# Gate stores, token loads and first weights put at other places of the queues in a fused attention and gated-FFN kernel

## The chip, the cores and the metric

The kernel runs on one NeuronCore of one Trainium2 chip. The metric is the time in microseconds that the device takes for one execution. A profiled execution of the kernel before, with its trace, is what the reading below rests on. Engines are named as the profile names them: PE (TensorE matmul), PEld (its weight loads), DVE (VectorE), ACT (ScalarE), POOL (GpSimd) and SP (SyncE, which here issues nearly all DMAs, one after the other, in the order of the program).

## The reference

```python
# q, k, v: (8, 12, 448, 64) f32; w_pre, w_post: (12, 12); w_in: (768, 2048); w_out: (2048, 768)
scores = matmul(q, k.T) / 8                          # per batch and head
scores = einsum('bhij,hg->bgij', scores, w_pre)      # heads mixed before the softmax
attn   = softmax(scores, axis=-1)
attn   = einsum('bhij,hg->bgij', attn, w_post)       # and after it
x      = matmul(attn, v) -> (3584 tokens, 768)
h      = x @ w_in                                    # 3584 x 2048
g      = h - tanh(h)
return g @ w_out                                     # 3584 x 768
```

## The kernel before, in words

The attention takes the first 870 us or so and is not touched. Its results go to memory as tiles `xs`. The two products of the FFN follow in seven token blocks of 512. Each factor is split into a high and a low part, and a product is the sum of three matmuls (high x high, high x low, low x high).

**Block 0** is done in the plain way: sixteen steps `Block0.step`, one for each 128 columns of `w_in` (f = 0 to 15). A step loads the weights of f + 2 into one of three buffers `w0`, runs 18 matmuls of 512 columns (`products`), and copies the bank out. Every second step the *gate* `g = h - tanh(h)` of the last two column groups goes on: the class `Gate` has ACT parts `a1` (u, qa), `a2` (t, qb), `a3` (qb again) and DVE parts `d1` (two instructions), `d2`, `d3` (which writes g). The result is stored to `go`. `load_all_xq` loads the *token tiles* b11l, b21l, t3l, b22l, t4l of the next pair of blocks.

**Blocks 1 to 6** are taken in three pairs s = 0, 1, 2 by a scheme with seven products in place of eight. `xq_jobs` is a generator of the *token sums*: it subtracts token tiles on DVE into `xr`, casts the high parts on ACT (`high`) and subtracts for the low parts on DVE (`low`); `next(xq)` does the next job. `pair_step(s, q, ...)` runs for q = 0 to 7; in it come seven products of nine matmuls each, with right sides b11, b21, t2, t1, t3, b22, t4, into two PSUM banks X and Y. I call the code around product i *slot i*. Product i first loads the weights of product i + 6 (`more_wa`, seven buffers `wa`), so that load waits until product i - 1 has read its buffer. X is written by products 0, 2, 4, 6, and Y by 1, 3, 5: product 4 adds onto X, and so waits until ACT has copied X out into h23 after product 2. `Late` holds the second half of the gate work of the step before, cut into v0 to v4, which stand in slots 0 to 4. The seven gate sums of a step are in one tile `g` with one buffer; they are stored to `gs` (1.75 MB) and the next step's v0 writes `g` again.

**The second product** (`w_out`) is cut into *units* of 12 matmuls (`Results`): 32 plain ones for block 0, then 56 for each pair. Units are called between the products (`res.units`); before a new weight tile or gate tile is used, its loads (`w2`, `gl`) are issued two ahead, and every second unit casts a gate tile into gh on ACT and gl on DVE (`parts`). HELD units are kept for the *joint* between two pairs, where there are no products of the first kind, and AHEAD units of the new pair are taken there in advance. At a joint v0 to v4 come one by one, each with one token-sum job and one unit.

Every engine carries out its instructions in the order in which the code calls them (`in_order`). The pools `plain` (w0 and the tokens xh, xl of block 0) are closed after block 0, and `wa`, `w2b` and `cb` take their place.

## Time and profile before

| | |
|---|---|
| three runs, median (range) | 1839.65 us (1835.8 to 1841.04) |
| the profiled execution: time, span of the core | 1841.15 us, 1839.4 us |
| busy: PE, PEld, DVE, ACT, POOL | 1696.6, 1410.8, 1215.5, 1148.1, 404.0 us |
| moved by DMA | 477.42 MB, 260 GB/s on the mean |
| DMA issues after the attention that are named below | gs<-g: 24 of 1792 KB; go<-g: 8 of 512 KB; w<-wi: 16 of 768 KB; wa: 168 of 384 KB |

The profile's times are microseconds from the start of the span. A row of the windows view gives for a stretch the busy time of each engine (with its number of instructions), then the granted clock of PE (1.00 is full speed), the share of DMA and its rate. A row of the timeline gives start, duration, engine, line, what is written and read, and in brackets how long the engine had been idle and what ended that. A row of the waits view gives who waited for whom: total, times, longest.

### The profile page before, as it was taken

The numbers are of one execution on the slowest core, as the hardware profiler recorded it, in microseconds if no ns is written. First come the engines' busy times: TensorE is split into PE (matmuls) and PEld (weight loads), VectorE is DVE, ScalarE is ACT, GpSimd is POOL, SyncE is SP. The second block draws the span as 40 slices with busy tenths as digits, with TensorE's granted clock in tenths as the row PEclk, the third lists the DMA queues.
The fourth block names the chain that finished last, engine by engine and source line by source line (L and its number), as shares of the span: only waits on it lengthen the run. The fifth ranks groups of instructions, "written<-read, shape, count | busy, mean of one in ns | idle before, by whom it ended". The sixth has DMA issues, their size and how long they took to land.

```text
span 1839.4 us, 40980 instructions
## 1 busy us (share of the span) xinstructions
PE 1696.6 (92%) x16068; PEld 1410.8 (77%) x16068; DVE 1215.5 (66%) x2119; ACT 1148.1 (62%) x2016; POOL 404.0 (22%) x574
## 2 busy tenths in 40 slices
PE   8999999999998999999776999789999699998998
PEld 6777777777776777777654888678888589888998
DVE  5676777666676677764365878848777857777333
ACT  5777877776887687775355666545666455665232
POOL 1354555454545455551000000000000000000000
PEclk9999999999999899999887999989999899999999
DMA  8768798787978689775556778787979779786997
GB/s 183 213 212 258 239 252 248 226 239 220 260 247 230 211 245 262 227 236 180 197 183 223 255 286 304 262 312 276 351 288 369 272 268 350 299 318 248 333 321 279
DMA packets 337743, 477.42 MB, mean 260 GB/s; under 512 B 103824, under 2 KB 262288, under 8 KB 337552
## 3 DMA queue, kind: packets, MB, share of 16 engines
q1 hardware_dynamic: 337244, 474.38, 78.2%
q8 instruction: 128, 2.10, 0.5%
q14 instruction: 63, 0.52, 0.1%
q10 hardware_dynamic: 308, 0.43, 0.1%
HBM read 277.09 MB, written 120.59 MB: 216 GB/s over the span
## 4 chain that ended last, share of the span: by engine, by line
PE 67%; DMA 12%; DVE 8%; ACT 6%; issue 3%; POOL 2%; SPq 2%; ACTq 0%; DVEq 0%; POOLq 0%
PE ps_o L929 12%; PE ps_m L971 8%; PE ps_p L890 7%; PE ps_h L315 6%; PE ps_h L316 6%; PE ps_h L318 5%; PE y L523 5%; PE ps_q L846 5%; PE y L525 5%; PE y L524 5%; DMA t<-s 2%; DMA gs<-g 2%; DMA w<-wo 1%; DMA vr<-in_v_dram 1%; PE ps_m L812 1%
## 5 line engine op out<-in xcount | busy, mean ns | idle before, releaser
L929 PEld LDWEIGHTS ps_o<-wr,e 60*112 60x112 f32 (+1 forms) x5760 | 307.7, 176 | 42.8 <-POOL wr L912 18.4
L929 PE MATMUL ps_o<-wr,e 60*112 60x60 f32 (+1 forms) x5760 | 316.4, 260 | 15.8 <-ACT at L939 7.0
L899 DVE TENSOR_REDUCE mx<-ps_p 128x1 f32<-128x448 f32 x360 | 207.9, 619 | 178.2 <-PE ps_p L890 177.8
L901 ACT ACTIVATE e<-ps_p,mx 128x448 f32<-128x448 f32 x360 | 225.4, 633 | 92.5 <-DVE mx L899 90.4
L523 PE MATMUL y<-w,gh 128*128 128x384 f32 x672 | 231.6, 345 | 39.8 <-DMA w<-wo 20.0
L525 PE MATMUL y<-w,gl 128*128 128x384 f32 x672 | 230.8, 343 | 7.2 <-DVE gl L438 7.2
L524 PE MATMUL y<-w,gh 128*128 128x384 f32 x672 | 230.0, 342 | 0.0
L438 DVE TENSOR_TENSOR gl<-gl,gh 128x1024 fp32r<-128x1024 f32 x92 | 112.6, 1224 | 172.3 <-ACT gh L437 172.2
L939 ACT COPY at<-ps_o 112x960 f32<-112x960 f32 x156 | 153.9, 987 | 82.7 <-PE ps_o L929 82.1
L890 PE MATMUL ps_p<-t,wpre 60*64 60x448 f32 (+1 forms) x1440 | 181.0, 570 | 13.2 <-DMA t<-s 11.0
L971 PEld LDWEIGHTS ps_m<-at,vr 112*64 112x64 f32 x3072 | 152.4, 140 | 34.6 <-ACT at L946 13.0
L971 PE MATMUL ps_m<-at,vr 112*64 112x120 f32 (+1 forms) x3072 | 167.2, 266 | 11.2 <-ACT at L946 5.2
L523 PEld LDWEIGHTS y<-w,gh 128*128 128x128 f32 x672 | 130.0, 193 | 46.6 <-ACT b22h L565 13.8
L437 ACT CAST gh<-gl 128x1024 fp32r<-128x1024 f32 x92 | 96.0, 1044 | 110.5 <-DMA gl<-gs 78.3
L912 POOL TENSOR_TENSOR wr<-wpost,zs 128x120 f32<-128x120 f32 x180 | 70.7, 393 | 329.6 <-DVE zs L911 226.5
L525 PEld LDWEIGHTS y<-w,gl 128*128 128x128 f32 x672 | 129.8, 193 | 8.7 <-DVE gl L438 8.6
L524 PEld LDWEIGHTS y<-w,gh 128*128 128x128 f32 x672 | 129.9, 193 | 3.7
L846 PE MATMUL ps_q<-kk,qh 64*120 64x448 f32 (+1 forms) x768 | 123.7, 399 | 1.2 <-DVE kk L798 0.5
L846 PEld LDWEIGHTS ps_q<-kk,qh 64*120 64x120 f32 (+1 forms) x768 | 59.9, 176 | 82.8 <-issue 51.4
L851 DVE COPY s<-ps_q 120x448 f32<-120x448 f32 (+1 forms) x192 | 112.5, 615 | 11.9 <-PE ps_q L846 10.6
L331 ACT ACTIVATE u<-h 128x1024 f32<-128x1024 f32 x56 | 59.5, 1063 | 95.7 <-DVE h L688 77.8
L347 ACT ACTIVATE qb<-u,bias 128x1024 f32<-128x1024 f32 x56 | 64.7, 1155 | 68.4 <-DVE qa L344 68.2
(174 smaller groups left out, 3349.1 us busy)
## 6 DMA issues: line engine op xcount, KB each, us to landing
t<-s SPq DMA_DIRECT2D x342, 210.0 KB
gs<-g SPq DMA_DIRECT2D x24, 1792.0 KB
gl<-gs SPq DMA_DIRECT2D x84, 512.0 KB
w<-wo SPq DMA_DIRECT2D x52, 768.0 KB
wa<-ss SPq DMA_DIRECT2D x96, 384.0 KB
w<-ts SPq DMA_DIRECT2D x48, 768.0 KB
wa<-wi SPq DMA_DIRECT2D x72, 384.0 KB
cr<-in_moe_w_in_dram SPq DMA_DIRECT2D x48, 256.0 KB
```

What stands on the lines that cost most here:

```text
L438: nc.vector.tensor_sub(lo, raw(lo), raw(hi))
L523: nc.tensor.matmul(y, gh[:, tok], wh, start=first, stop=False, skip_group_check=True)
L524: nc.tensor.matmul(y, gh[:, tok], wl, start=False, stop=False, skip_group_check=True)
L525: nc.tensor.matmul(y, gl[:, tok], wh, start=False, stop=last, skip_group_check=True)
L846: nc.tensor.matmul(ps[:n, :S], qx[a, hp, :], kx[a, hp % 2], start=(x == 0), stop=(x == 2))
L851: eng(sts[i][:n, 2 * hp + j, :], ps[:n, :S])
L890: nc.tensor.matmul(pss[r][halves[j], :], wpre[k, :], ts[j][k, :], start=True, stop=True)
L899: nc.vector.tensor_reduce(out=mx, in_=ps, axis=AX.X, op=ALU.max, negate=True)
L901: nc.scalar.activation(e, ps, AF.Exp, bias=mx, scale=1.0, accum_out=zs[:, 0, r : r + 1])
L929: nc.tensor.matmul(ps[:CP, j, c * GP : (c + 1) * GP].rearrange("p (h i) -> p h i", i=GI)[:, :, r * GH : (r + 1) * GH], e[k, c * CP : (c + ...
L939: nc.scalar.copy(ats[i0][:, :, :, at : at + 2 * GI].rearrange("p c h (j i) -> p j (c h) i", j=2), ps[:CP, :, : NC * GP].rearrange("p j (x ...
L971: nc.tensor.matmul(pv[j * D : (j + 1) * D, r, :n], vt[:, j, c, :], ats[i][:, c, 2 * hp + j, :n], start=(c == 0), stop=(c == NC - 1),)
```

## The change

1. *Block 0:* the store of a gate to `go` is no longer issued in its own step but in the next one, behind that step's weight load (`self.store`); two more steps are issued ahead of the flush that ends the attention; the token loads are spread over the steps f = 3 to 7, the loads of w2 and gl over f = 10 to 15, the token sums over even f from 6 (five jobs, where there were seven); the new pools are opened right behind the matmuls of f = 15, with `w2b` at the first place and `wa` behind it.
2. *Every pair step:* `copy_predicated` is cut off from `d3` as `d4`; v3 (a3 and d3) now stands in slot 2 ahead of the copy of X, d4 of the second half in slot 3, the sums in slots 3 and 4; the store to `gs` is issued in slot 6.
3. *Joints:* the gate parts come first and the token sums behind them; five of eleven token-sum jobs are done there, and the other six in slots 0 to 4 of the pair's first step (two in slot 0); the store of the last `g` comes after ten units; AHEAD is 6 instead of 4, and each of seven places has two units; `int(due + 1e-6)` mends the rounding of the units.

```diff
     def close_plain():
         ff.plain.close()
-        ff.wap, ff.w2b, ff.cb = pool("wa", 7, "left"), pool("w2b", 1, "left"), pool("cb", 9, "left")
+        ff.w2b, ff.wap, ff.cb = pool("w2b", 1, "left"), pool("wa", 7, "left"), pool("cb", 9, "left")
...
         def d3(self, out):
             nc.vector.tensor_mul(out, self.qa, self.u)
+
+        def d4(self, out):
             nc.vector.copy_predicated(out, self.qb.bitcast(I32), self.t)
...
-        def step(self):
+        def step(self, between=None):
...
             if f + 2 < NF:
                 load_w0(f + 2)
+            if self.store:
+                self.store()
+                self.store = None
+            if between:
+                between(f)
             if f < NF:
                 ph = hbank()
                 products(ph, ff.w.pop(f), [ff.x[c] for c in range(NK)], True, True)
+                if f == NF - 1:
+                    close_plain()
+                    more_wa(6)
...
-                    nc.sync.dma_start(gos[:, f - 3 : f - 1], g)
+                    old.d4(g)
+                    self.store = lambda: nc.sync.dma_start(gos[:, f - 3 : f - 1], g)
...
         sub("t3l", "b11l")
+        yield
         both("b11")
...
         low("t1", xr)
+        yield
         sub("b22l", xr)
...
         def v2(self):
             self.g2.d1()
+
+        def v3(self):
             self.g2.d2()
-
-        def v3(self):
+            self.g2.a3()
+            self.g2.d3(self.g[:, 2:4])
+
+        def v4(self):
             g = self.g
-            self.g2.a3()
-            self.g2.d3(g[:, 2:4])
+            self.g2.d4(g[:, 2:4])
             nc.vector.tensor_add(g[:, 4:6], g[:, 0:2], g[:, 2].unsqueeze(1).to_broadcast([P, 2, TB]))
 
-        def v4(self):
+        def v5(self):
             g = self.g
             nc.vector.tensor_add(g[:, 6], g[:, 1], g[:, 4])
             nc.vector.tensor_add(g[:, 2], g[:, 3], g[:, 6])
-            nc.sync.dma_start(gss[self.s][:, :, self.q], g)
+
+        def store(self):
+            nc.sync.dma_start(gss[self.s][:, :, self.q], self.g)
...
         product(2, X, False)
         if late:
             late.v2()
+            late.v3()
         h23 = work("h23")
         nc.scalar.mul(h23[:, 0], X, -1.0)
...
         g1.a3()
+        if late:
+            late.store()
         rest(6)
...
+        for _ in range(2):
+            block0.step()
         now()
...
-    load_all_xq(0, ("b11l", "b21l", "t3l", "b22l", "t4l"))
...
+    def between0(f):
+        if 3 <= f <= 7:
+            load_all_xq(0, (("b11l", "t3l", "b21l", "b22l", "t4l")[f - 3],))
+        if f in (10, 12):
+            res.more_w2((f - 10) // 2)
+        if f in (13, 15):
+            res.more_gr((f - 13) // 2)
+        if 6 <= f < NF and f % 2 == 0:
+            next(xq, None)
+
     while block0.f < NF + 2:
-        block0.step()
-        if 3 <= block0.f < NF + 1 and block0.f % 2:
-            next(xq, None)
-        if block0.f == NF - 2:
-            res.more_w2(1)
-        if block0.f == NF:
-            close_plain()
-            more_wa(6)
+        block0.step(between0)
+    block0.store()
     res.more_w2(2)
-    res.more_gr(1)
...
-    HELD, AHEAD = 8, 4
+    HELD, AHEAD = 8, 6
...
             def between(i):
-                next(xq, None)
+                for _ in range(1 + (i == 0)):
+                    next(xq, None)
...
-        for f in (late.v0, late.v1, late.v2, late.v3, late.v4):
-            f()
-            next(xq, None)
-            res.units(1)
+        jobs = [
+            [late.v0], [late.v1, late.v2], [late.v3], [late.v4], [late.v5, partial(next, xq, None)],
+            [partial(next, xq, None)] * 2 + [late.store], [partial(next, xq, None)] * 2,
+        ]
+        for fs in jobs:
+            for f in fs:
+                f()
+            res.units(2)
         late = None
-        if s + 1 < NS:
-            for _ in range(HELD + AHEAD - 5):
-                next(xq, None)
-                res.units(1)
```

On SP at the start of block 0 the order before is as follows (xs<-x is the last store of the attention, w<-wi a weight load of block 0, here that of f = 3; the first gate's store comes three rows further down).

```order
L738 DMA xs_64<-x 768x1x208
L556 DMA b11l<-xs_58 128x3x384
L556 DMA b11l<-xs_59 128x3x128
L556 DMA b21l<-xs_58 128x3x384
L556 DMA b21l<-xs_59 128x3x128
L556 DMA t3l<-xs_59 128x3x320
L556 DMA t3l<-xs_60 128x3x192
L556 DMA b22l<-xs_59 128x3x320
L556 DMA b22l<-xs_60 128x3x192
L556 DMA t4l<-xs_58 128x3x384
L556 DMA t4l<-xs_59 128x3x128
L308 DMA w_13433<-wi_66 128x1536
```

With the change the same queue holds:

```order
L308 DMA w_13397<-wi_66 128x1536
L308 DMA w_13419<-wi_67 128x1536
L760 DMA xs_64<-x 768x1x208
L308 DMA w_13473<-wi_67 128x1536
L567 DMA b11l<-xs_58 128x3x384
L567 DMA b11l<-xs_59 128x3x128
L308 DMA w_13503<-wi_68 128x1536
L388 DMA go<-g 128x1024
L567 DMA t3l<-xs_59 128x3x320
L567 DMA t3l<-xs_60 128x3x192
L308 DMA w_13540<-wi_68 128x1536
```

The weight loads of f = 3 and 4 moved ahead of the attention's last store, the five token tiles stand one by one behind a weight load each, and the store to go stands behind one.

In a pair step (s = 0, q = 3) SP and ACT read before, first SP from the weight loads of slots 3 and 4 to the store, then ACT from slot 0 to slot 3:

```order
L613 DMA wa_14339<-ss3_80 128x768
L613 DMA wa_14355<-ss3_80 128x768
L644 DMA gs0_90<-g_14286 896x1x512
L613 DMA wa_14386<-ss3_80 128x768
L613 DMA wa_14404<-ss3_80 128x768
```

```order
L663 COPY h01_14450<-ps_h_14437 128x512
L331 ACTIVATE u_14453<-h23_14323 128x1024
L332 ACTIVATE qa_14454<-u_14453,bias_13124 128x1024
L336 ACTIVATE t_14472<-h23_14323 128x1024
L337 ACTIVATE qb_14471<-u_14453,bias_13124 128x1024
L678 ACTIVATE h23_14489<-ps_h_14437 128x512
L347 ACTIVATE qb_14471<-u_14453,bias_13124 128x1024
L684 ACTIVATE h01_14450<-ps_h_14438 128x512
```

and with the change (names as before; lines have moved by 9 to 20):

```order
L626 DMA wa_14341<-ss3_80 128x768
L626 DMA wa_14355<-ss3_80 128x768
L626 DMA wa_14385<-ss3_80 128x768
L626 DMA wa_14403<-ss3_80 128x768
L663 DMA gs0_90<-g_14286 896x1x512
```

```order
L682 COPY h01_14450<-ps_h_14437 128x512
L331 ACTIVATE u_14453<-h23_14325 128x1024
L332 ACTIVATE qa_14454<-u_14453,bias_13124 128x1024
L336 ACTIVATE t_14472<-h23_14325 128x1024
L337 ACTIVATE qb_14471<-u_14453,bias_13124 128x1024
L347 ACTIVATE qb_14471<-u_14453,bias_13124 128x1024
L698 ACTIVATE h23_14491<-ps_h_14437 128x512
L704 ACTIVATE h01_14450<-ps_h_14438 128x512
```

The store moved behind the weight loads of slots 5 and 6, and on ACT a3 (the second qb) moved ahead of the copy of X into h23.

At the first joint DVE reads with the change, from the old pair's v0 (d3, d4) on; rows L572 and L579 are token sums, L449 the low part of a gate tile:

```order
L353 COPY_PREDICATED g<-qb,t 128x1024
L449 TENSOR_TENSOR gl<-gl,gh 128x1024
L340 SCALAR_TENSOR_TENSOR qa<-qa,h_15152 128x1024
L341 TENSOR_TENSOR t<-h_15152,t 128x1024
L344 SCALAR_TENSOR_TENSOR qa<-qb,qa 128x1024
L350 TENSOR_TENSOR g<-qa,u 128x1024
L449 TENSOR_TENSOR gl<-gl,gh 128x1024
L353 COPY_PREDICATED g<-qb,t 128x1024
L655 TENSOR_TENSOR g<-g 128x1024
L659 TENSOR_TENSOR g<-g 128x512
L660 TENSOR_TENSOR g<-g 128x512
L572 TENSOR_TENSOR xr<-t3l,b11l 128x1536
```

Before, three token-sum rows (L561, L568) stood between v0's last row and the second half's d1; now none stands there, and the rows of t2, t4, t3 and b22 follow inside the next pair step.

More of the change, by code (lines that the diff above doesn't have):

```diff
@@ L356, in __init__ @@
         def __init__(self):
-            self.f, self.old = 0, None
-        def step(self):
+            self.f, self.old, self.store = 0, None, None
+        def step(self, between=None):
             f, old = self.f, self.old
@@ L625, in v0 @@
             self.g1.d3(self.g[:, 0:2])
+            self.g1.d4(self.g[:, 0:2])
         def v1(self):
@@ L682, in pair_step @@
         if late:
-            late.v3()
+            late.v4()
         nc.scalar.mul(h01[:, 0], Y, -1.0)
@@ L689, in pair_step @@
         if late:
-            late.v4()
+            late.v5()
         g1 = Gate(h01)
@@ L1305, in kernel_body @@
                 due += per_step / 7
-                units.append(int(due))
-                due -= int(due)
+                units.append(int(due + 1e-6))
+                due -= units[-1]
             late = pair_step(s, p, late, units, between)
```

## The prediction

> **What bounds the kernel now.** I read the engines' busy time, then windows by stage, then what PE waited for, then the queues there.
>
> ```profile
> PE 1696.6 (92%) x16068; PEld 1410.8 (77%) x16068; DVE 1215.5 (66%) x2119; ACT 1148.1 (62%) x2016; POOL 404.0 (22%) x574
> 888.40:1015.67 127.27, 87.14 (x334) 69.30 (x334) 75.42 (x59) 67.41 (x71) 0.00 (x0) 0.81 0.59 209
> 1015.67:1160.27 144.60, 143.23 (x684) 119.35 (x683) 119.59 (x117) 93.43 (x102) 0.00 (x0) 1.00 0.80 287
> 1160.27:1239.03 78.76, 58.05 (x280) 51.89 (x279) 44.83 (x36) 35.81 (x47) 0.00 (x0) 0.87 0.80 280
> 1239.03:1420.76 181.73, 181.73 (x899) 162.94 (x899) 140.53 (x136) 112.39 (x128) 0.00 (x0) 1.00 0.87 319
> 1420.76:1496.54 75.78, 55.78 (x268) 50.80 (x267) 49.29 (x44) 31.34 (x30) 0.00 (x0) 0.89 0.80 288
> 1496.54:1678.24 181.70, 181.70 (x899) 162.91 (x899) 138.89 (x135) 113.68 (x132) 0.00 (x0) 1.00 0.82 301
> 1678.24:1839.40 161.16, 144.18 (x793) 141.82 (x791) 62.03 (x64) 47.76 (x55) 0.00 (x0) 0.96 0.85 303
> ```
>
> PE bounds it. The seven stretches are: the entry (block 0 from f = 3, and the first step of pair 0); pair 0's other seven steps, up to the end of their last product; joint 1 with the first step of pair 1; pair 1's other steps; joint 2 with a first step; pair 2's other steps; joint 3 to the end. In the pairs' steps PE is full; it idles 40 us at the entry and 21, 20 and 17 at the joints, and there its clock is low besides. No matmul goes away, so all gain must come from these four places, and the full steps can only lose. Pair 0's row has 69 groups (a product, or a unit of as many columns): 143.23 / 69 = 2.08 us a group, and twice that, 4.1, for the 18 matmuls of a block-0 product.
>
> ```profile
> PE ps_h L315 <- DMA w<-wi: 22.0, 4, 10.2
> PE ps_h L315 <- DMA wa<-wi: 13.5, 1, 13.5
> 881.42 1.75 SPq L556 DMA_DIRECT2D b11l<-xs  x2
> 889.49 2.27 SPq L308 DMA_DIRECT2D w<-wi  x3
> 898.58 0.77 PE L315 MATMUL ps_h<-xh,w 128*128 128x512 f32 x1 [10.17 <-DMA w<-wi]
> 947.96 0.32 SPq L377 DMA_DIRECT2D go<-g  x1
> 948.37 1.21 SPq L308 DMA_DIRECT2D w<-wi  x2
> 953.71 0.76 PE L315 MATMUL ps_h<-xh,w 128*128 128x512 f32 x1 [5.12 <-DMA w<-wi]
> 981.39 0.32 SPq L377 DMA_DIRECT2D go<-g  x1
> 981.82 1.20 SPq L613 DMA_DIRECT2D wa<-wi  x2
> 986.27 0.76 PE L315 MATMUL ps_h<-b11h,wa 128*128 128x512 f32 x1 [13.49 <-DMA wa<-wi]
> ```
>
> The large entry waits have one form: SP stands at a store whose gate is not done, or at five token loads, and the weight load behind it goes out late; alone it lands 5.3 us after its issue (948.37 to 953.71).
>
> **The entry.** Ahead of the stores, a weight load goes out when its buffer has been read, two products (8.2 us) before it is needed. It can still queue behind a token load and a gate store: 768 + 768 + 512 KB at the 319 GB/s of the fullest row are 6.6 us, with issue and landing about 8. So nearly all 22.0 go; I leave 4 us of waits on the 13 products. The first `wa` load stands behind the gate of f = 10, 11, which is done about 1 us after product 14; the load lands some 7 us after that product, 3 after the last. The first pair step's product 0 then starts at 888.4 + 13 x 4.1 + 4 + 3 = 949 against 986.27.
>
> But that step has lost its cover: ACT and DVE still owe two gates, and six token-sum jobs have moved into it. The rows that price this, and the ring of the next part:
>
> ```profile
> L565 ACT CAST t2h<-xr x2: 1471/1476/1482, 1185.2 to 1443.8; 128x1536 fp32r<-128x1536 f32 x2
> L568 DVE TENSOR_TENSOR t2l<-xr,t2h x2: 1751/1752/1753, 1188.9 to 1447.6; 128x1536 fp32r<-128x1536 f32 x2
> L438 DVE TENSOR_TENSOR gl<-gl,gh 128x1024 fp32r<-128x1024 f32 x92 | 112.6, 1224 | 172.3 <-ACT gh L437 172.2
> L437 ACT CAST gh<-gl 128x1024 fp32r<-128x1024 f32 x92 | 96.0, 1044 | 110.5 <-DMA gl<-gs 78.3 <-PE y L524 26.5 <-DMA gl<-go 3.1
> 1095.51 0.53 SPq L644 DMA_DIRECT2D gs<-g  x1
> 1103.03 1.23 DVE L350 TENSOR_TENSOR g<-qa,u 128x1024 f32<-128x1024 f32 x1 [3.06 <-DMA gs<-g]
> 1104.36 1.06 ACT L331 ACTIVATE u<-h 128x1024 f32<-128x1024 f32 x1 [2.73 <-DVE g L350]
> 1104.36 1.41 DVE L351 COPY_PREDICATED g<-qb,t 128x1024 f32<-128x1024 int32 x1
> 1106.63 1.23 DVE L340 SCALAR_TENSOR_TENSOR qa<-qa,h 128x1024 f32<-128x1024 f32 x1 [0.29 <-ACT qa L332]
> 1108.91 1.22 DVE L344 SCALAR_TENSOR_TENSOR qa<-qb,qa 128x1024 f32<-128x1024 f32 x1
> 1109.09 0.60 ACT L678 ACTIVATE h<-ps_h 128x512 f32<-128x512 f32 x1 [0.49 <-DVE t L341]
> 1109.74 0.50 PE L315 MATMUL ps_h<-t3h,wa 128*128 128x512 f32 x1 [0.83 <-ACT h L678]
> 1110.17 1.15 ACT L347 ACTIVATE qb<-u,bias 128x1024 f32<-128x1024 f32 x1 [0.48 <-DVE qa L344]
> 1115.38 0.84 PE L318 MATMUL ps_h<-b22h,wa 128*128 128x512 f32 x3
> ```
>
> A gate costs DVE 3 x 1.22 + 1.23 + 1.41 = 6.3 us, and two of them in turn with ACT's parts end about 11 us after product 15. t2's low part (1.48 on ACT, 1.75 on DVE) comes behind: product 2 waits 6.5. The unit behind it needs gl, which stands on DVE behind t2's and t4's low parts and two subtractions of 1.75 each: 5.5. t3 is cast only when product 3 is copied out: 0.6 + 1.48 + 1.75 = 3.8 ahead of product 4. b22 is cast behind slot 4's a1: a subtraction of 0.7, 1.06, 1.15, 1.48 and 1.75 make 6.1, less a unit of 2.08: 4. Together 19.8, and 4 for slow clock: the step lasts 20.8 + 23.8 and ends at 993 or 994, not 1015.67. **Entry: -22.** Bounds: -33 (half of the step's waits gone) and -10 (weight loads still late by 4 us every third time).
>
> **Pair 0's steps: the store.** Here the change adds a wait. There is a ring: d3 (L350) cannot write g before the store has landed, 7.5 us after its issue; u waits for d3, and so on to ACT's copy of X (L678), for which product 4 (t3) waits. Before, product 4 comes 6.7 us after d3 starts. The change moves both ends. First, a3 (L347) now stands ahead of the copy, and itself waits for d2 (L344): copy and product come at 1110.17 + 1.15 + 0.6 instead, 8.85 after d3. Second, the store goes out behind slot 6's weight load, which waits for the end of product 5 (b22): 1115.38 + 0.84 - 1109.74 = 6.5 after product 4 starts, and 0.5 for issue. The ring is 8.85 + 6.5 + 0.5 + 7.5 = 23.4 us; PE's step of ten groups is 20.8. From the second store on, product 4 waits 2.6 in each of six steps: 15.6, less the 1.4 idle of before. The clock adds:
>
> ```profile
> 1696.24:1699.65 3.41, 1.37 (x9) 1.05 (x8) 2.49 (x3) 0.00 (x0) 0.00 (x0) 1.00 0.24 89
> 1699.65:1703.07 3.42, 3.42 (x12) 3.42 (x11) 0.00 (x0) 0.00 (x0) 0.00 (x0) 0.50 1.03 370
> ```
>
> 2.04 us of idle within 3.41 were followed by 3.42 at half clock. By the place of a 2.6 us wait in such a stretch about 6 in 10 would do so, at 1.7 us inside the ring: some 5. **+19.5.** Bounds: 0 (the store lands sooner than in the rows above) and +30 (a landing of 9.7, below).
>
> The Trainium skill ("TensorE: Matmul & The Clock Gate", section "Why this matters for your kernels") has it that PE idle below about 3 us does not lower the clock; by it the clock would add nothing here. The two rows above speak against it.
>
> **Pairs 1 and 2.** A step has 12 or 13 groups, 25 to 27 us, so the ring has room, but not in each step. Where a unit stood in slot 4, product 5 ends 10 groups into its step: 20.9 + 0.5 + 7.5 less 25 is d3 at 4 us into the next. Where gl is made in slot 0 there, casts and sums (1.04 + 1.22 + 0.7) push the copy of X to 11.8 after d3; in slot 1, behind ACT's t and qb, to 13.2. Product 4 is due after 7 groups, at 14.6. By the order two steps of a pair then wait 1.2 and two 2.6; with the clock 9.5. Two units fewer stand in these steps (-4.2): **+5.3 for each pair.** Bounds: -4 and +13.
>
> **The joints.**
>
> ```profile
> PE y L523 <- DMA w<-wo: 13.6, 1, 13.6
> PE y L523 <- ACT qb L337: 8.7, 1, 8.7
> PE y L525 <- DVE gl L438: 5.1, 3, 3.6
> ```
>
> At joint 1 (first row) a pair's last store waits on SP ahead of the next weights; at joint 2 (the others) v0 and the token sums alternate on DVE, and PE waits. Now that store is behind the loads, and DVE makes four gl among ten gate instructions and four sums: 24.6 us from d3, which starts 6 us after the last product; the loads behind eight output stores hold the last two units to about 34. PE has 15 groups, 31 us. So the next pair's product 0 comes 38 us after the last product, against 78.8 - 25 = 53.8. Its first step has the t3 and b22 waits of the entry, partly under units: 25 + 8.4, and 2 for clock. **Joint 1: 73.3 for 78.8, -5.5; joint 2 by the same sum 73, -2.8** (it has three units more than before). Joint 3 has no token sums: of 17 us idle and some 5 of slow clock 16 stay, and one unit goes: **-8.** All three together could give -30 (no idle left) or +5 (weights still late).
>
> Loads and sums that only change places cost the same; the cover is block 0's matmuls, and its price without them is the entry's lower bound. The pools' new order only changes which buffer a load waits for: the first two `wa` then wait for f = 13 in place of 15, which is in the 3 us above.
>
> **The sum.** -22 + 19.5 - 5.5 + 5.3 - 2.8 + 5.3 - 8 = -8: 1833 us against the profiled execution's 1841.15 (span 1839.4). The median of the runs is 1.5 lower: **1832**. What a measurement of this kernel tells from no change is 0.3%, 5.5 us.
>
> **The rivals.**
> - *The store lands later still (slower).*
>
> ```profile
> 1414.67 0.53 SPq L644 DMA_DIRECT2D gs<-g  x1
> 1424.33 1.23 DVE L350 TENSOR_TENSOR g<-qa,u 128x1024 f32<-128x1024 f32 x1 [2.48 <-DMA gs<-g]
> ```
>
> Here, with token loads around it, it took 9.7. Each us of landing costs six steps of pair 0 and eight of the others, 14 us. At 9.1 it is +22: 1854; from 8.1 on there is no gain. For it: two weight loads now stand straight ahead of the store. Against it: the 7.5 above had two right behind. 0.23.
> - *The loads stay the bound (no change).* DMA is already 0.80 to 0.87 busy in the pairs; if the joints give half and block 0's loads come 1.5 us later each second time, 1840. 0.24.
> - *The ring does not bind,* because the store lands while DVE is busy anyway: pair 0 at 0, the others at -4 each: 1795 to 1804. The 3.06 of wait ahead of d3 speaks against it. 0.09.
> - *Short waits leave the clock alone:* 5 + 2 x 2.3 + 2 less: 1820. The page named above gives this rule. 0.08.
>
> **The numbers.** The forecast's own case (1815 to 1846) has 0.36. Faster: 0.31 of it, the last two rivals, and 0.04 of the second: 0.52. No change: 0.18 of the second, 0.04 of the first case and 0.02 of the store's: 0.24. Slower: the rest, 0.24. The range, 1804 to 1855, reaches the rivals on both sides.
>
> **What would show it.** Right: product 0 near 950; idle ahead of t2, t3 and b22 in each pair's first step; 2 to 3 us ahead of t3, ended by ACT's copy, in six steps of pair 0, with d3 waiting for gs; product 0 some 38 us behind the last product at joints 1 and 2. Wrong: steps of pair 0 still 20.8 long, or weight loads of block 0 still waited for by 5 us and more.

## Result, and the profile after

The changed kernel takes 1882.2 us (median of four runs, 1879.1 to 1885.1) against 1839.65 for the kernel before, the median of its three runs (a fourth, disturbed one took 3230 us and is left out): a ratio of 1.0236, 95% interval 1.0204 to 1.0267. It is 2.4% slower, where 1832 was forecast and 1855 was the upper end. The profiled execution took 1885.07 us (span 1883.3), 43.9 more than the one of before. The page's line of busy times, the windows of the same seven stretches (columns as in the prediction), and the waits of PE from f = 3 on (smaller rows left out):

```profile
PE 1724.8 (92%) x16068; PEld 1419.0 (75%) x16068; DVE 1214.6 (64%) x2119; ACT 1146.1 (61%) x2016; POOL 403.4 (21%) x574
```

```profile
891.66:1000.28 108.62, 86.51 (x334) 67.19 (x333) 75.60 (x60) 68.25 (x72) 0.00 (x0) 0.87 0.71 253
1000.28:1167.17 166.89, 149.85 (x684) 123.45 (x683) 119.37 (x116) 93.17 (x102) 0.00 (x0) 0.96 0.74 256
1167.17:1248.18 81.01, 65.83 (x303) 56.99 (x303) 46.06 (x36) 36.49 (x47) 0.00 (x0) 0.85 0.76 269
1248.18:1445.39 197.21, 183.65 (x875) 161.40 (x875) 137.74 (x134) 110.05 (x127) 0.00 (x0) 0.97 0.82 293
1445.39:1528.23 82.84, 64.69 (x303) 57.83 (x303) 52.16 (x46) 34.94 (x37) 0.00 (x0) 0.90 0.78 277
1528.23:1725.60 197.37, 183.88 (x875) 161.36 (x875) 137.65 (x134) 110.19 (x127) 0.00 (x0) 0.97 0.77 274
1725.60:1883.30 157.70, 139.12 (x780) 135.73 (x779) 60.82 (x63) 46.61 (x54) 0.00 (x0) 0.98 0.86 300
```

```profile
PE ps_h L315 <- ACT h L698: 37.2, 15, 5.1
PE y L534 <- DMA w<-wo: 14.0, 6, 5.8
PE y L534 <- ACT gh L448: 12.1, 3, 7.9
PE ps_h L315 <- ACT b22h L576: 10.6, 3, 4.4
...
PE ps_h L315 <- DMA w<-wi: 3.4, 3, 1.4
```

The entry is shorter: block 0's weight loads are waited for 3.4 us in place of 22.0. But the pairs' steps, full before, are so no longer. The largest wait is now on L698, ACT's copy of X, ahead of product 4. By the prediction's steps, in us against before:

| step | forecast | measured |
|---|---|---|
| entry, to the end of the first pair step | -22 | -15.4 (1000.28 for 1015.67) |
| pair 0, steps 1 to 7 | +19.5 | +22.3 |
| joint 1 and first step | -5.5 | +2.3 |
| pair 1, steps 1 to 7 | +5.3 | +15.5 |
| joint 2 and first step | -2.8 | +7.1 |
| pair 2, steps 1 to 7 | +5.3 | +15.7 |
| joint 3 to the end | -8 | -3.5 |
| sum | -8 | +43.9 |

The timeline of one long step (step 3 of pair 1) shows the way from the store to product 4. The columns are start, duration, engine, line and operation; in brackets the idle time before it and what ended it.

```profile
1293.44 0.32 SPq L428 DMA_DIRECT2D gl<-gs  x1
1293.81 0.42 SPq L418 DMA_DIRECT2D w<-ts  x1
1295.52 0.32 SPq L626 DMA_DIRECT2D wa<-ss  x1
1295.93 0.56 SPq L663 DMA_DIRECT2D gs<-g  x1
...
1306.45 1.23 DVE L350 TENSOR_TENSOR g<-qa,u 128x1024 f32<-128x1024 f32 x1 [5.69 <-DMA gs<-g]
...
1307.77 1.06 ACT L331 ACTIVATE u<-h 128x1024 f32<-128x1024 f32 x1 [5.29 <-DVE g L350]
...
1317.70 1.15 ACT L347 ACTIVATE qb<-u,bias 128x1024 f32<-128x1024 f32 x1 [4.76 <-DVE qa L344]
1318.75 0.58 ACT L698 ACTIVATE h<-ps_h 128x512 f32<-128x512 f32 x1
...
1319.38 0.79 PE L315 MATMUL ps_h<-t3h,wa 128*128 128x512 f32 x1 [5.10 <-ACT h L698]
```

The store goes out at 1295.93; d3 (L350) stands ready on DVE for 5.69 us and starts when the store has landed, 10.5 us after its issue; u (L331) waits for d3; a3 (L347) and behind it the copy (L698) come 11.3 and 12.3 us after d3, and PE has stood 5.10 us. In the list of what waited for the store's line, the changed kernel's row comes first, then the row of the kernel before (us, times).

```profile
  DVE g L350: 73.4, 21
```

```profile
  DVE g L350: 18.8, 14
```

### The profile page after: what moved, and what is told of

It reads as the page before. It is cut to its first block, busy times and chain, and to the rows that moved or that the text cites. A ratio compares the mean times of both kernels' runs of the same rounds, so it can differ in the third digit from the quotient of the medians.

```text
span 1883.3 us, 40937 instructions
## 1 busy us (share of the span) xinstructions
PE 1724.8 (92%) x16068; PEld 1419.0 (75%) x16068; DVE 1214.6 (64%) x2119; ACT 1146.1 (61%) x2016; POOL 403.4 (21%) x574
## 4 chain that ended last, share of the span: by engine, by line
PE 57%; DMA 17%; DVE 10%; ACT 9%; issue 3%; SPq 2%; POOL 2%; ACTq 0%; DVEq 0%; POOLq 0%
PE ps_o L951 12%; DMA gs<-g 8%; PE ps_m L993 7%; PE ps_p L912 7%; PE ps_q L868 5%; PE ps_h L315 4%; PE ps_h L316 4%; PE ps_h L318 4%; PE y L534 3%; PE y L536 3%; PE y L535 3%; DMA t<-s 2%; DMA w<-wo 2%; DMA vr<-in_v_dram 1%; DVE gl L449 1%
## 5 line engine op out<-in xcount | busy, mean ns | idle before, releaser
L951 PE MATMUL ps_o<-wr,e 60*112 60x60 f32 (+1 forms) x5760 | 319.0, 261 | 15.7 <-ACT at L961 7.0
L449 DVE TENSOR_TENSOR gl<-gl,gh 128x1024 fp32r<-128x1024 f32 x92 | 112.5, 1224 | 178.7 <-ACT gh L448 175.0
L961 ACT COPY at<-ps_o 112x960 f32<-112x960 f32 x156 | 153.8, 986 | 84.1 <-PE ps_o L951 83.5
L993 PEld LDWEIGHTS ps_m<-at,vr 112*64 112x64 f32 x3072 | 150.4, 139 | 31.2 <-ACT at L968 12.4
L331 ACT ACTIVATE u<-h 128x1024 f32<-128x1024 f32 x56 | 59.5, 1062 | 163.5 <-DVE h L708 83.1
L534 PEld LDWEIGHTS y<-w,gh 128*128 128x128 f32 x672 | 129.7, 193 | 37.7 <-ACT gh L448 23.9
L347 ACT ACTIVATE qb<-u,bias 128x1024 f32<-128x1024 f32 x56 | 64.5, 1152 | 104.6 <-DVE qa L344 104.6
```

The source lines that it names most:

```text
L449: nc.vector.tensor_sub(lo, raw(lo), raw(hi))
L534: nc.tensor.matmul(y, gh[:, tok], wh, start=first, stop=False, skip_group_check=True)
L951: nc.tensor.matmul(ps[:CP, j, c * GP : (c + 1) * GP].rearrange("p (h i) -> p h i", i=GI)[:, :, r * GH : (r + 1) * GH], e[k, c * CP : (c + ...
L961: nc.scalar.copy(ats[i0][:, :, :, at : at + 2 * GI].rearrange("p c h (j i) -> p j (c h) i", j=2), ps[:CP, :, : NC * GP].rearrange("p j (x ...
L993: nc.tensor.matmul(pv[j * D : (j + 1) * D, r, :n], vt[:, j, c, :], ats[i][:, c, 2 * hp + j, :n], start=(c == 0), stop=(c == NC - 1),)
```

## Experiments

Measured medians, ratios to the kernel before on the same chip with 95% intervals, and, from one profile of each, the length of the stretches in us: entry (from block 0's first product to the end of the first pair step), steps 1 to 7 of each pair, and joints 1 and 2 each with the first step behind it. Pairs 1 and 2 hold 899 matmuls in the kernel before, e4 and e8, 863 in e13 and 875 in the others; 12 are one unit, 2.1 us.

| kernel | us | ratio | entry | pair 0 | pair 1 | pair 2 | joint 1 | joint 2 |
|---|---|---|---|---|---|---|---|---|
| before | 1840 | 1 | 145.4 | 144.6 | 181.7 | 181.7 | 78.8 | 75.8 |
| changed | 1882.2 | 1.0236 [1.0204, 1.0267] | 127.0 | 166.9 | 197.2 | 197.4 | 81.0 | 82.8 |
| e1 | 1830.9 | 0.9950 [0.9923, 0.9977] | 123.9 | 152.2 | 180.1 | 180.1 | 81.9 | 82.9 |
| e2 | 1855.4 | 1.0074 [1.0039, 1.0108] | 125.9 | 149.2 | 193.1 | 190.8 | 79.5 | 83.1 |
| e3 | 1824.0 | 0.9899 [0.9838, 0.9960] | 127.3 | 145.2 | 177.4 | 177.4 | 83.4 | 84.4 |
| e4 | 1884.0 | 1.0245 [1.0199, 1.0290] | 142.1 | 149.6 | 189.6 | 201.4 | 84.1 | 83.6 |
| e5 | 1823.2 | 0.9928 [0.9901, 0.9955] | 121.9 | 148.6 | 179.4 | 179.4 | 81.2 | 83.0 |
| e6 | 1796.8 | 0.9781 [0.9753, 0.9809] | 121.4 | 145.0 | 177.4 | 177.4 | 75.4 | 74.7 |
| e7 | 1814.9 | 0.9881 [0.9855, 0.9908] | 116.2 | 144.9 | 177.5 | 177.4 | 83.4 | 83.0 |
| e8 | 1819.7 | 0.9915 [0.9883, 0.9946] | 123.8 | 144.8 | 182.1 | 182.6 | 76.9 | 80.5 |
| e9 | 1797.9 | 0.9780 [0.9749, 0.9811] | 117.0 | 145.1 | 177.4 | 177.4 | 75.0 | 78.9 |
| e10 | 1802.0 | 0.9804 [0.9776, 0.9833] | 120.3 | 145.0 | 177.5 | 177.4 | 75.2 | 75.3 |
| e11 | 1786.6 | 0.9726 [0.9698, 0.9754] | 116.5 | 142.2 | 177.5 | 177.5 | 73.7 | 75.6 |
| e12 | 1793.9 | 0.9757 [0.9722, 0.9791] | 116.9 | 145.1 | 177.4 | 177.4 | 73.8 | 76.2 |
| e13 | 1864.6 | 1.0139 [1.0096, 1.0181] | 123.7 | 168.0 | 188.7 | 189.2 | 78.4 | 84.3 |
| e14 | 1784.6 | 0.9692 [0.9664, 0.9720] | 115.7 | 142.2 | 177.4 | 177.5 | 72.7 | 75.7 |

Stretches that PE fills agree to 0.1 us between kernels; entry and joints with the same code differ by 4 to 5, so there a single profile tells only larger differences. The kernel before had medians of 1837.6 to 1839.7 beside these runs.

### The ring: e1 to e5

**e1, store in slot 4 again.**

```diff
             late.v5()
+            late.store()
         g1 = Gate(h01)
...
         g1.a3()
-        if late:
-            late.store()
```

> The changed kernel with one thing undone: in a pair step the gate store goes out behind v5 in slot 4 again, not behind slot 6's weight load. Ring theory: the chain store, landing, d3, copy of X, product 4 no longer binds, as the store leaves 4 to 6 us earlier; pair 0's seven steps go from 166.9 back to about 145, pairs 1 and 2 from 197 to about 180 each; in all 50 to 55 us less, about 1828. Rival, the order on ACT alone (a3 ahead of the copy of X): the waits ahead of t3 stay at 2 us or more in most steps and less than 15 us come back, 1867 or more. Rival, loads: the store stands on SP ahead of the weight loads again, and these become late: less than 30 us come back, and waits for wa appear in the steps.

Measured 1830.9, 51 us less than the changed kernel: the ring theory's number. But pair 0 came back to 152.2 only, and from pair 0 to joint 3 PE still waited 10.8 us for the copy of X: with a3 ahead of the copy the ring still touches some steps.

```profile
PE ps_h L315 <- ACT h L698: 10.8, 8, 2.7
```

**e2, copy of X ahead of v3 again.**

```diff
             late.v2()
-            late.v3()
         h23 = work("h23")
         nc.scalar.mul(h23[:, 0], X, -1.0)
+        if late:
+            late.v3()
```

> The changed kernel with one thing undone: in slot 2, v3 (d2, a3, d3) stands behind ACT's copy of X again. Store still behind slot 6's weight load. Ring theory: the chain from d3 to product 4 is 2.2 us shorter (6.7 for 8.9), so each of the 16 or so binding steps gives back 2.2 us and some slow clock: 35 to 45 us less, about 1843. Rival, the store alone (its landing waits on the DMA queues): under 15 us less. Rival, ACT's order alone: as good as with the store moved too, 50 us and more.

Measured 1855.4: 27 us back, less than the 35 to 45 expected. Pair 0 gives back 17.7, as a ring shorter by 2.2 us in each step should; pairs 1 and 2 only 4.1 and 6.5. In pair 1 the waits on the copy fell from 11.5 us, the changed kernel's row,

```profile
PE ps_h L315 <- ACT h L698: 11.5, 5, 5.1
```

to the 4.2 of e2, where another wait came in, for a unit's gh, which is cast on ACT too; and PE's busy time stayed (183.44 us, 183.65 in the changed kernel), so the slow clock gave nothing back:

```profile
PE ps_h L315 <- ACT h L697: 4.2, 2, 2.9
PE y L534 <- ACT gh L448: 3.6, 1, 3.6
PE ps_h L315 <- DVE h L688: 1.6, 1, 1.6
```

**e3, both undone.**

> The changed kernel with both undone: store behind v5 in slot 4, v3 behind the copy of X. Ring theory: the same as with the store alone, within 5 us, because the ring no longer binds and the rest of the step is full: about 1828. Rival, ACT's order: clearly faster (10 us and more) than with the store alone.

Measured 1824.0, 16 us faster than the kernel before; beside e1, 6.9 less by the medians, between the two expectations. The windows of its pair 0 and pair 1 show PE full, but for 1.9 us in pair 0, at clock 1.00:

```profile
1000.79:1145.98 145.19, 143.28 (x684) 119.39 (x683) 118.68 (x116) 92.74 (x102) 0.00 (x0) 1.00 0.78 284
1229.37:1406.80 177.43, 177.43 (x875) 158.68 (x875) 137.82 (x134) 111.21 (x127) 0.00 (x0) 1.00 0.85 316
```

Against it the changed kernel's pair 1 is 19.8 us longer: 197.21 - 183.65 = 13.6 of idle, and 183.65 - 177.43 = 6.2 for the same 875 matmuls at a lower clock. The two moves add to more than their sum: a3 alone +6.9 (e1), the store alone +31.4 (e2), both +58.2. The intervals of e1 and e3 overlap, but the three pairs' stretches together say the same: +12.3, +33.0 and +61.4.

**e4, the kernel before with the late store alone** in its pair steps, as e1's diff the other way round.

> The kernel before with one part of the change alone: in the pair steps the gate store goes out behind slot 6's weight load (the joints keep their order). Ring theory: 6.7 + 6.5 + 0.5 + 7.5 to 10 = 21.2 to 24.7 us for a ring, against a step of 20.8 in pair 0 and 25 to 27 in pairs 1 and 2: 3 to 9 us more in pair 0, 0 to 10 in the others, in all 5 to 20 us slower, about 1852. Rival, the store has no part in it (a3's place has): no difference, 1840.

Measured 1884.0: 44 us slower than before, where 5 to 20 were expected. One line of the change, by itself, costs as much as the whole change on balance. (The upper end of the expected ring adds up to 23.7 us, not 24.7.) Pair 0 lost 5.0 and pair 1 7.9, as foreseen, but pair 2 19.7; why so much more than pair 1 stays open. And the joints, which I had left out, lost 5.3 and 7.9. There the pair's last-but-one store lands 12.4 us after its issue, d3 and so the last store come late, and in this old order that store still stands ahead of the next weight loads; the first row of PE's waits at joint 1:

```profile
PE y L523 <- DMA w<-wo: 20.2, 1, 20.2
```

**e5, a second buffer.** The late store and a3 stay as changed; the slots that d3 writes first get a tile with two buffers. To make room, `wa` has six buffers in place of seven and is loaded five products ahead.

```diff
-            self.g = work("g", 7)
+            self.ga = ff.ga.tile([P, 2, TB], F32, name="ga", tag="ga")   # a pool of two
+            self.gb = work("gb", 5)
...
-            nc.sync.dma_start(gss[self.s][:, :, self.q], self.g)
+            nc.sync.dma_start(gss[self.s][:, 0:2, self.q], self.ga)
+            nc.sync.dma_start(gss[self.s][:, 2:7, self.q], self.gb)
```

> The changed kernel, store still behind slot 6's weight load and a3 still ahead of the copy of X, but the first two of g's seven slots (what d3 writes first) in a tile of its own with two buffers; the other five in one buffer, two stores for one; six wa buffers for seven, loaded five products ahead, to make room. Ring theory: d3 has nothing to wait for, pair 0's steps come back to 145 to 150 and pairs 1 and 2 to about 180 us each: about 1835. Rival, the landing is not what holds the steps (a3's place on ACT, or the loads that stand around the store): less than 20 us come back, 1862 or more.

Measured 1823.2: 59 us less than the changed kernel. On SP the stores keep their place behind slot 6's weight load, but d3 no longer waits for any of them, and the pairs are nearly full again. So it is the buffer that the store holds, not the store's place as such. The windows of pairs 0 and 1:

```profile
987.81:1136.43 148.62, 144.94 (x684) 120.31 (x683) 120.28 (x117) 93.67 (x102) 0.00 (x0) 0.99 0.84 289
1217.59:1396.94 179.35, 177.74 (x875) 158.57 (x875) 138.69 (x135) 110.15 (x127) 0.00 (x0) 1.00 0.88 317
```

### What sets the landing: e13

In the changed kernel 21 stores are followed by a d3 that stood waiting for them. Sorted by what SP had issued in the 4 us ahead of the store, the time from issue to d3's start was 7.7 to 9.0 us behind one weight load (384 KB, 13 stores), 9.8 and 10.5 behind 1664 KB, 11.1 and 11.5 behind 2048, 12.0 and 12.5 behind more; of the two left, one took 8.6 behind 1280 KB and one 11.1 behind 1152. In the kernel before nearly all stores had nothing ahead and up to 4096 KB issued behind them before they landed, and those that d3 waited for took 7.5 to 7.9 (but for the one of 9.7). That one, and the one of 11.1 behind 1152 KB, stand among token loads; the bytes just ahead do not account for these two. Nor do they give the landing closely: in e4's profile five stores behind 1664 and 2048 KB took 9.6 to 11.4. e13 tests this: slot 5's units, with their loads, go behind the store.

```diff
-            res.units(units[i])
+            res.units(0 if i == 5 else units[5] + units[6] if i == 6 else units[i])
```

> The changed kernel as it is (late store, one g buffer, a3 ahead), with slot 5's units and their loads (gl 512 KB, w 768 KB) put into slot 6, behind the store. Only weight loads of 384 KB then stand just ahead of a store. If the loads ahead set the landing: every store of the pairs' steps lands in 7.7 to 9.0 us, the steps that followed landings of 10.5 to 12 get 2 to 4 us shorter and lose some slow clock, pairs 1 and 2 take about 187 us each for 197, in all about 1862. Rival, the place in the step or the traffic behind the store sets it: landings of 10 to 12 us stay in the same steps, and the time stays at 1882.

Measured 1864.6, 18 us less, where 1862 was expected. The stores of pair 1's steps now land in 7.7 to 8.9 us up to the last step's (10.7). The same store as in the timeline above (on SP, then d3 on DVE):

```profile
1289.21 0.32 SPq L626 DMA_DIRECT2D wa<-ss  x1
1289.63 0.56 SPq L663 DMA_DIRECT2D gs<-g  x1
1290.24 0.65 SPq L428 DMA_DIRECT2D gl<-gs  x1
```

```profile
1297.85 1.22 DVE L350 TENSOR_TENSOR g<-qa,u 128x1024 f32<-128x1024 f32 x1 [1.16 <-DMA gs<-g]
```

8.2 us in place of 10.5, with 1.3 MB behind it rather than ahead. With the unit that has moved out of the stretch added (2.1), pair 1 takes 190.8 for 197.2. (The move also puts those units' casts of gh and gl later on ACT and DVE; what that is worth was not separated.)

### Entry and joints: e6 to e8

All three stand on e3.

**e6, two token-sum jobs a slot** in each pair's first step.

```diff
-                for _ in range(1 + (i == 0)):
+                for _ in range(2):
```

> The changed kernel with both undone (store in slot 4, copy of X ahead), and in each pair's first step two token-sum jobs a slot, so that t3 and b22 are made two slots before they are needed. If these sums, made only one slot ahead, hold the first steps: 39.4 us become about 32 in pairs 1 and 2, 48.8 become about 45 in pair 0, in all 12 to 18 us less than the 1824 of both undone: about 1809. Rival, DVE and ACT are full there whatever the order, and the wait moves to t2 and gl: no difference beyond 5 us.

Measured 1796.8, less than e3 by 27 us by the medians and by 22 by the ratios, above the 12 to 18 expected. The waits of PE in the first step of pair 1, e3 and then e6 (its window begins with the joint's last units):

```profile
PE ps_h L315 <- ACT b22h L576: 4.4, 1, 4.4
PE y L534 <- DMA w<-wo: 1.5, 1, 1.5
PE ps_h L316 <- DVE t3l L579: 1.3, 1, 1.3
PE ps_h L315 <- ACT t3h L576: 1.0, 1, 1.0
PE ps_h L316 <- DVE b22l L579: 1.0, 1, 1.0
```

```profile
PE y L534 <- DMA w<-wo: 1.8, 1, 1.8
PE y L534 <- ACT c L544: 1.2, 1, 1.2
PE y L536 <- DVE gl L449: 0.2, 1, 0.2
```

The t3 and b22 waits, 7.7 us, are gone, and the step (39.4 us in e3) is 30.6 long: the sums had been made one slot too late.

**e7, one job in each block-0 step.**

```diff
-        if 6 <= f < NF and f % 2 == 0:
+        if 6 <= f < NF:
```

> The changed kernel with both undone, and in block 0 one token-sum job in each step from f = 6 on, not in every second one: ten of eleven are then out of the way before pair 0. If the missing cover of the sums is what the first step pays for: entry and first step 127 us become about 112, in all about 1810. Rival, DVE's work in block 0 (51 of 78 us busy) then holds the gates and so the banks and stores: block 0 grows by what the first step gains, 1820 to 1830.

Measured 1814.9: the entry is 11 us shorter (127.3 to 116.2). The first step falls from 48.8 to 29.9, block 0 grows from 78.5 to 86.3; so the rival had a part, but not the whole.

**e8, joints 1 and 2 in the old order**, joint 3 as changed.

```diff
-    HELD, AHEAD = 8, 6
+    HELD, AHEAD = 8, 4
...
+            for f in (late.v0, late.v1, (late.v2, late.v3), late.v4, (late.v5, late.store)):
...
+                next(xq, None)
+                res.units(1)
```

> The changed kernel with both undone, and joints 1 and 2 as before the change (all token sums there, alternating with the last gates, store behind v4, 12 units), joint 3 as changed. My forecast had the new joints worth 8.3 us, and the two units more in each 4.2 per pair: by it this kernel is some 17 us slower, about 1840. Theory now, from the stretches: joint and first step together took 83.4 and 84.4 us in the new order and 78.7 and 75.8 in the old, so the old ones gain 13 and pay 8.4 for the units: about 1819.

Measured 1819.7: about e3 (the intervals overlap), as expected from the stretches. The old joints take 10.4 us less in the sum of both, the two units more in each pair cost 9.8. The new order of the joints, by itself, gained nothing.

### A faster kernel: e9 to e12, e14

**e9** is e6 and e7 together.

> Both undone, with two token-sum jobs a slot in the first steps and one in each block-0 step from f = 6: the last two edits together. If they add up: entry and first step 116 us (as with the sums in block 0), the other first steps 30 us: 1797 - 5 = 1792. Rival: sums in block 0 make it longer by what the first step of pair 0 has left to give: 1797, no difference.

Measured 1797.9, as e6 (1796.8): the gains did not add. The entry is 4.4 shorter than e6's, joint 2 and the end longer by 4 each, where the code is the same.

**e10** is e9 with fewer jobs in block 0.

```diff
-        if 6 <= f < NF:
+        if 8 <= f < NF:
```

> The same with the sums in block 0 from f = 8, eight of eleven jobs there, three in the first two slots of pair 0. Block 0 grew from 78.5 to 86.3 us with ten jobs and from 5; if that growth is DVE's late gates, eight jobs give block 0 about 82 and the first step about 31: 113 in place of 116, 3 us less than with ten. Rival: the three jobs left cost the first step more than block 0 gains: 3 us more.

1802.0 against 1797.9: not better, though the intervals overlap. The profile shows the rival's way: the first step (35.9 us, 32.2 in e9) pays for the jobs left to it, and block 0 (84.4 for 84.8) hardly gains.

**e11** is e9 with the late store of the change and e5's two buffers.

> As with the sums from f = 6 and two a slot, copy of X ahead, but with the change's late store (behind slot 6's weight load), the ring opened by two buffers for g's first two slots. It tells what the late store is worth when nothing waits for its landing. Theory: nothing in the pairs, where no product waited for a weight load with the early store either; the pairs' steps stay at 145.0, 177.4, 177.4, the time within 5 us of the kernel with the early store. Rival, the change's own idea: weight loads ahead of the store come sooner at the joints, where units wait 9 us for w: 5 us or more less.

1786.6 against e9's 1797.9: 11 us less, where at most 5 were expected. Pair 0 is 142.2, full to the last matmul, where 145.1 with the early store has a trace of the ring in it; pairs 1 and 2 are the same 177.4. From block 0 on its profile is 9.9 us shorter than e9's: 2.9 of it in pair 0, the rest in joints 1 and 2 (1.2 and 3.3), end (2.0) and entry (0.5), each no more than the same code differs by; so beyond pair 0 the gain is not placed. The rival's reason is not borne out: PE's waits for `w<-wo` were 32 us in e11's profile, 22 in e9's.

**e12** is e9 with one load moved.

```diff
-                    for x, at in (("b11l", 0), ("b21l", 1), ("t3l", 4), ("b22l", 5), ("t4l", 6)):
+                    for x, at in (("b11l", 0), ("b21l", 1), ("t3l", 4), ("b22l", 5)):
...
             res.units(2)
+            if fs is jobs[1] and s + 1 < NS:
+                load_all_xq(s + 1, ("t4l",))
```

> As with the sums from f = 6 and two a slot, early store, and the token loads of t4 (1.1 MB) at joints 1 and 2 issued after the joint's first four units, no longer in slot 6 of the pair's last step. If the 9 us that the joints' units wait for w are the queue behind store and token loads: product 0 comes 3 to 4 us earlier at each joint, 6 to 8 us less in all. Rival: t4's sum is then late, or w waits for its buffer: no difference or a few us more.

(t4's loads are 768 KB a pair; the 1.1 MB was a slip.) 1793.9 against 1797.9, within what the runs spread: product 0 came 5.8 and 2.5 us earlier at the joints, and the first step of pair 1 took 4.6 longer. Unsettled.

**e14** is e11 with e12's move.

> The late store with two buffers for g's first two slots, copy of X ahead, sums from f = 6 and two a slot, and t4's token loads after the joint's first four units. If the gains of the two last edits add: 1787 - 4 = 1783. Rival, the joint is bound by the weight loads of its units alone and t4's loads only come between them later: 1787, no difference.

1784.6 against e11's 1786.6: no difference to be told. It is the fastest of all: ratio to before 0.9692, 3.1% faster. Its pair 1:

```profile
1198.38:1375.82 177.44, 177.44 (x875) 158.70 (x875) 138.25 (x134) 110.88 (x127) 0.00 (x0) 1.00 0.88 317
```

## Why the prediction was wrong, step by step

By the table of the result the forecast misses by 52 us: 20.6 in pairs 1 and 2, 22.2 at the three joints, 6.6 at the entry and 2.8 in pair 0. Two terms of the sum failed. The landing of a store was put at 7.5 us, and in pairs 1 and 2 it took up to 12.5. And the slow clock was put far too low wherever PE waits often: the sum had 4 us for it in the first step of pair 0, 2 at each of joints 1 and 2 and 1.9 in each of pairs 1 and 2; measured were 11.6, 9.6 and 8.5, and 6.2 and 6.5 (PE's busy time less that of the same matmuls at full clock).

**Entry: right in the mechanism, the clock too small.** Product 0 came 78.5 us after block 0's first product, against 78.7 forecast; by the clock 951.70 for 949, as attention ended 3 us later (870 and 873; in all profiles here, 862 to 878). The first step was 48.6 us, not 44.6. Its idle, 48.58 - 32.36, was 16.2, less than my 19.8; but I had put 4 us for slow clock, and PE was busy 32.4 for 20.8 of work: 11.6. Part of the reason stands in the last section: a window at half clock with more than some 0.7 us of idle was always followed by another. The row of the step:

```profile
951.70:1000.28 48.58, 32.36 (x99) 23.80 (x100) 25.92 (x21) 19.67 (x20) 0.00 (x0) 0.72 0.45 155
```

**Pair 0: right.** Idle 17.0 (forecast 15.6), busy 149.85 against e3's 143.28: 6.6 for the clock (forecast 5). (The terms of that forecast, 15.6 - 1.4 + 5, add up to 19.2, not 19.5.) The six waits ahead of product 4 were 2.6 to 3.2 us long.

**Pairs 1 and 2: the step of the ring that failed,** and most of it the term that the prediction called the landing. I took 7.5 us, from stores of the kernel before with loads right behind them, and held that against the rival of a later landing. Loads behind a store did not delay it (but for the one of 9.7 us); loads ahead did. The change put the store behind whatever the slot-5 unit and slot 6 had issued, and in pairs 1 and 2 that is up to 2048 KB, with token loads 2624: 7.9 to 12.5 us. e13 takes these loads away and gets back 6.4 in pair 1. What stays, 190.8 against 177.4, is 13.4; my sum had 9.5 there (5.3, and the 4.2 of the two units). So of the 10 us missed in each pair some 6 are the landing and 4 the rest of the sum, and 3 of these 4 are the clock: in e13 pair 1 idled 8.7 us where I had 7.6, and its 863 matmuls took 5.0 longer than at full clock where I had 1.9.

The Trainium skill ("DMA: Bandwidth & Descriptors", section "Queues, rings and completion order") says that on each DMA engine descriptors are consumed in ring order, with one ring per engine for all that SP issues. By that rule, bytes issued ahead count and bytes behind don't; the rows above agree (9.8 and 10.5 us behind 1664 KB, 7.5 to 7.9 behind none), but for the two stores among token loads.

**Joints 1 and 2: too hopeful by 8 and 10.** I counted 31 us of units and loads that hold the last two to 34, and set product 0 at 38 us. It came 42.9 and 43.5 us behind the last product, and 44 in e3, where no landing holds d3. PE's work there took longer and waited for weights at more than one place, as e3's window from the last product of pair 0 to the next product 0, and its waits there, show:

```profile
1145.98:1190.01 44.03, 36.25 (x180) 32.33 (x180) 26.86 (x21) 19.41 (x27) 0.00 (x0) 0.88 0.94 325
```

```profile
PE y L504 <- DMA w<-wo: 5.9, 2, 3.4
PE y L534 <- DMA w<-wo: 1.9, 1, 1.9
```

44.0 - 36.3 = 7.8 us of idle, all of it for w, and some 5 of slow clock in 36.3 of busy time for my 31. The first step behind it was 38.2 and 39.4, not 35.4: the same t3 and b22 waits as forecast, 7.7 us, and again a clock dearer than my 2. In all the idle of joint 1 and its first step was what I had summed, 81.0 - 65.8 = 15.2 us against 15.1; what failed there is the clock, 65.8 of busy time for 56.2 of work (31.2 for the 15 units, 25 for the step). Joint 2 had 8.5 of clock and 18.2 of idle, 3 more than my sum; its largest wait was for a unit's gh on ACT, 7.9 us.

**Joint 3: -3.5, not -8.** PE still waited for w, up to 5.8 us at once.

**The rivals.** "The store lands later still" is the one that came, with 0.23, but hardly in pair 0, whose first six stores landed in 7.7 to 8.3 us. Its 1854 stopped at 9.1 us in the mean, and had no joints in it. "Loads stay the bound" fell for block 0. "The ring does not bind" fell with e5. "Short waits leave the clock alone" fell too:

```profile
1031.13:1034.54 3.41, 0.82 (x4) 0.48 (x3) 3.27 (x3) 2.12 (x3) 0.00 (x0) 1.00 0.47 124
1034.54:1037.96 3.42, 3.42 (x9) 2.62 (x8) 1.79 (x3) 0.00 (x0) 0.00 (x0) 0.50 0.00 0
...
1106.22:1109.64 3.42, 1.96 (x9) 1.30 (x7) 3.39 (x4) 1.85 (x3) 0.00 (x0) 1.00 0.56 179
1109.64:1113.05 3.41, 1.93 (x8) 1.61 (x9) 3.27 (x3) 1.91 (x3) 0.00 (x0) 1.00 0.96 361
1113.05:1116.46 3.41, 3.41 (x19) 2.90 (x18) 2.34 (x4) 1.76 (x2) 0.00 (x0) 1.00 0.73 234
```

A wait of 2.59 us ahead of product 4 lies within one window of 3.41 us (0.82 busy; the windows are those of the clock, see the last section), and the next window runs at half clock. One of 2.94, three steps later, falls 1.46 and 1.48 into two windows, and the clock stays. Three of pair 0's six waits were of the first kind (1.99 us of idle in one window was the least), three of the second. The rule of the Trainium skill ("TensorE: Matmul & The Clock Gate", section "Why this matters for your kernels"), no idle gap above about 3 us, would have let the 2.59 us pass; the measurement decides.

## What to carry to other kernels

Before a store is moved later, find what writes its buffer next and follow that round to the store again: if the ring is longer than the step, each step pays the difference and a lower clock on top. Price its landing with the bytes that stand ahead of it on the queue in its new place, not with a landing seen in the old one. Where the ring is too long, a second buffer for the part that is written first (here two slots of seven) opens it; the late store then cost nothing, and work moved out of a joint must be ready a slot or two before it is used, or it waits in the open there. And where PE waits often, price the slow clock from busy times in such a stretch of the trace, not from one wait.

## What was not expected of the hardware

A store of 1792 KB landed in 7.5 to 7.9 us with up to 4096 KB issued behind it before it landed (but for one of 9.7, among token loads), and in 11 to 12.5 with 2 to 2.6 MB issued in the 4 us ahead of it in the changed kernel.

The granted clock changes only on a fixed grid of 3.413 us: all 668 changes in the sixteen profiles lie within 0.004 us of one, each profile with its own. What goes with a change is PE's idle time in the window of that grid just before it. From 888 us on, each of the 161 windows at full clock with 1.95 us or more of idle was followed by one at half clock, and none with less than 1.44; between the two 25 windows were followed by half clock, and others were not. Back to full clock takes more: of the windows at half clock, the 188 that were followed by full clock had at most 0.69 us of idle, and the 145 that were followed by another at half had at least 0.61. So steps of pair 0 with waits of 2.6 to 3.0 us took 23.6 to 23.9 us or 25.1, by where the wait fell; and the first step of pair 0, with eight waits of 1.1 to 4.2 us on casts and low parts, ran at a mean clock of 0.72.
